# Decay attention and two expert layers on one core: weights' splitting paced by a count of VectorE's work, stores on GpSimd's queue, another order of the first expert layer's steps

## The chip, the cores and the metric

One NeuronCore of a Trainium2 chip runs the whole kernel. The metric is the device time of one execution in microseconds (us). The engines are named as in the profile: PE (TensorE), DVE (VectorE), ACT (ScalarE), POOL (GpSimd), SP (SyncE, which here only issues DMAs).

## What is computed

```python
def reference(q, k, v, s, w_in, w_out, w1, w2, w3, w_out2):       # cut
    scores = q @ k.T / sqrt(64)                  # 4 x 8 heads, 576 tokens, 64 wide
    cum = cumsum(max(s, 0));  bias = min(-(cum_i - cum_j), 0)
    attn = softmax(where(causal, -1e9, scores + bias)) @ v
    x = attn as (2304 tokens, 512)
    h = max(x @ w_in, 0)                         # 512 -> 2048
    x = (h * h) @ w_out                          # 2048 -> 512
    h = max(x @ w1, x @ w2, x @ w3)              # 512 -> 768 each
    return h @ w_out2                            # 768 -> 512
```

The weights arrive as 64-bit floats, the rest in 32 bits.

## The kernel before, in words

The order of every engine's instructions is the order in which the code emits them. There are three stages.

**Attention** works on 16 pairs of heads. A pair has nine units (tiles of scores), and a table (`ORDER`) says which step of which unit is emitted at each turn: scores on PE, mask and row maximum on DVE (line 673), exponential on ACT (line 687), transposes on PE and their copies on ACT (lines 729 to 754), the product with `v` on PE (line 774, tile `xv`), the row factors through DRAM (`r`, `px`, lines 704 to 713), the multiplication by them on POOL (line 792, tile `ax`) and the store of the pair's result on POOL's DMA queue (line 797, `x_at`). SP issues the loads of `xk`, `xq`, `ck`, `cq`, `xv`, and the small DMAs of `r` and `px`. Towards the end, `first_op` loads the first tokens of the next stage (`fx`, line 804), and ACT and DVE split them into a high and a low part (lines 810, 813); `FIRST_RAW` and `FIRST_OPS` say how many units ahead of the end of attention each of this is emitted.

**The weights** are prepared in jobs, by a class `Slots`, beside the attention and the first expert layer. A block of 128 x 512 64-bit words is loaded into a stage tile (`st`, line 379, two half loads), and four DVE operations of 512 elements (lines 386, 391, 395, 399) turn each word into a rounded 32-bit number and its rest; line 406 adds them. Where a layer uses sums of weights (a scheme with seven products in place of eight, lines 448 to 450), two blocks make one `sums` tile of seven parts. ACT makes the high part (lines 457, 419), DVE (POOL in attention) the low part by subtraction (lines 461, 422), and both are stored in DRAM (`keep_p`, lines 469 and 471; `keep`, line 426). PE's weights are then loaded from there into slots `sl` (lines 495, 498) by SP. A job is a list of stages; after each step of the main loop `pump` lets the open jobs go on by a credit of about one operation per step, whatever that operation's length. Weights' loads and stores are issued by SP in attention and by POOL after it (`queue`).

**The first expert layer** goes through 24 items; an item is a group of 768 tokens and a pair of blocks of the 2048 inner columns. It has seven products `p` (i = 0, 3, 2, 1, 4, 5, 6; six matmuls of 384 columns each, line 818) into two PSUM banks in turn (`first` in the trace), and eight output pieces `o` (three matmuls of 512 and three of 256 columns, line 1045), which belong to the item before. In `after`, ACT copies the banks after i = 0, 2, 1 into a tile `rr` (line 1006), DVE adds the banks after i = 3, 4, 5 to it (line 1017, called the rr addition below), ACT takes the maximum with zero, squares, and rounds to the high part (lines 1000, 996, 810), and DVE subtracts it for the low part (line 813, tile `hh`), which is emitted right behind the step. A product needs its bank read by the ACT or DVE operation of two products earlier, and an output piece needs both parts of `hh`. The products and pieces alternate:

```python
    for n in range(2, len(items1)):
        for c, i in enumerate(IN_ORDER):
            add_p(n, i)
            add_o(n - 1, pieces[c])
        add_o(n - 1, pieces[7])
```

**The second expert layer** and the output products (lines 818 and 1248) follow. No weights are prepared in it.

## Time and profile before

| | us |
|---|---|
| median of the two timed runs | 924.52 (923.7 and 925.33) |
| the profiled execution, its own time | 923.03 |
| its span in the trace | 921.3 |
| attention (to PE's last product of it) | 196.3 |
| first expert layer | 196.3 to 641.5 |
| second expert layer and output | 641.5 to 921.3 |

The 1.7 us between the profiled time and the span lie around the traced instructions. The stages are set apart by PE's products: its last product with the transposed row sums (line 777) starts at 196.1, its first products of the second expert layer at 640.1 and 641.5.

### The profile page before, as it was taken

The page shows a single profiled execution, that of the slowest core. Times are in us where ns is not written, and L with a number is a line of the kernel's source. Part 1 is how long each engine was busy: PE and PEld are TensorE (multiplying, and loading weights), DVE is VectorE, ACT ScalarE, POOL GpSimd, SP SyncE. Part 2 cuts the span into 40 slices and gives each one's busy share as a digit, 9 for nine tenths or more (in the row PEclk, how much of TensorE's full clock was granted, in tenths as well). Part 3 has the DMA queues.
Part 4 walks back from the last instruction along what each step waited for, and adds up shares of the span by engine and source line. Part 5 has one row for each costly group of instructions (what it writes and reads, how often), then busy time and mean ns, then how long its engine had stood idle before and what let it go on. Part 6 is the DMA issues. An engine that isn't in the chain of part 4 may idle for free.

```text
span 921.3 us, 16001 instructions
## 1 busy us (share of the span) xinstructions
PE 843.3 (92%) x5766; PEld 727.9 (79%) x5766; DVE 631.3 (69%) x1330; ACT 469.7 (51%) x981; POOL 182.8 (20%) x288
## 2 busy tenths in 40 slices
PE   8999968788887888989999989998799999999998
PEld 4655544467777877878999978986799999999998
DVE  7878758645876877777767776688245764676356
ACT  6898956755543544555555645553223442443224
POOL 2234241353132433322222212321000000000000
PEclk9999988988997999999999999999899999999999
DMA  4666867759786999945789837797983378246822
GB/s 145 201 180 214 274 190 246 226 160 386 243 298 238 345 320 354 334 166 201 263 289 329 303 105 259 248 385 273 384 306 144 113 277 278 96 144 194 315 71 69
DMA packets 89461, 220.28 MB, mean 239 GB/s; under 512 B 13480, under 2 KB 38120, under 8 KB 89384
## 3 DMA queue, kind: packets, MB, share of 16 engines
q1 hardware_dynamic: 69008, 150.06, 48.4%
q0 software_dynamic: 20352, 69.22, 20.6%
q8 instruction: 45, 0.74, 0.3%
q14 instruction: 32, 0.26, 0.1%
q10 hardware_dynamic: 24, 0.01, 0.0%
HBM read 158.22 MB, written 61.00 MB: 238 GB/s over the span
## 4 chain that ended last, share of the span: by engine, by line
PE 48%; DVE 18%; DMA 14%; ACT 8%; issue 8%; SPq 3%; POOL 2%; DVEq 0%; ACTq 0%; POOLq 0%
PE first L818 14%; PE banks L818 12%; PE banks L1045 7%; PE banks L1248 6%; DMA xq<-in_qT_dram 3%; PE pairs L774 3%; DVE xs L813 2%; DMA sl<-keep_p 2%; DMA st<-in_w_in_dram 2%; DVE rr L1017 2%; DMA px<-r 2%; DVE sums L448 1%; DVE sums L461 1%; DVE hh L813 1%; ACT xs L810 1%
## 5 line engine op out<-in xcount | busy, mean ns | idle before, releaser
L818 PE MATMUL first<-xs,sl 128*128 128x384 f32 x1350 | 279.5, 344 | 43.8 <-DVE rr L1017 27.4
L818 PEld LDWEIGHTS first<-xs,sl 128*128 128x128 f32 x1350 | 232.8, 191 | 51.5 <-DVE rr L1017 28.4
L1045 PE MATMUL banks<-hh,sl 128*128 128x512 f32 (+1 forms) x1152 | 235.3, 344 | 4.6 <-ACT hh L810 3.7
L1045 PEld LDWEIGHTS banks<-hh,sl 128*128 128x128 f32 x1152 | 199.5, 192 | 35.9 <-ACT hh L810 5.4
L818 PE MATMUL banks<-xs,sl 128*128 128x384 f32 x720 | 138.5, 338 | 0.2 <-DVE pt L1051 0.2
L818 PEld LDWEIGHTS banks<-xs,sl 128*128 128x128 f32 x720 | 125.7, 190 | 1.3 <-DVE c L1172 0.8
L1000 ACT ACTIVATE rr<-rr 128x384 f32<-128x384 f32 x69 | 36.3, 525 | 155.4 <-DVE rr L1017 155.4
L813 DVE TENSOR_TENSOR hh<-rr,hh 128x384 fp32r<-128x384 f32 (+1 forms) x69 | 47.7, 691 | 65.4 <-ACT hh L810 65.2
L687 ACT ACTIVATE e<-e,nm 128x128 f32<-128x128 f32 (+2 forms) x144 | 83.7, 585 | 16.9 <-DVE nm L673 16.7
L1248 PE MATMUL banks<-sl,hh 128*128 128x256 f32 x513 | 70.1, 283 | 1.7 <-DVE hh L813 1.4
L1248 PEld LDWEIGHTS banks<-sl,hh 128*128 128x128 f32 x513 | 66.8, 189 | 3.1 <-DVE hh L813 2.3
L774 PE MATMUL pairs<-et,xv 128*64 128x320 f32 (+4 forms) x448 | 56.5, 386 | 8.1 <-DMA xv<-in_v_main_dram 6.4
L774 PEld LDWEIGHTS pairs<-et,xv 128*64 128x64 f32 (+1 forms) x448 | 29.6, 142 | 42.2 <-issue 11.8
L1172 DVE TENSOR_TENSOR c<-banks,c 128x384 f32<-128x384 f32 x45 | 25.0, 555 | 47.1 <-PE banks L818 47.1
L813 DVE TENSOR_TENSOR xs<-xr,xs 128x768 fp32r<-128x768 f32 x44 | 42.7, 971 | 17.7 <-ACT xs L810 17.3
L729 PEld LDWEIGHTS pairs<-identF,e 64*128 64x128 f32 x800 | 35.4, 146 | 19.9 <-ACT et L751 8.8
L729 PE MATMUL pairs<-identF,e 64*128 64x64 f32 x800 | 42.8, 236 | 8.8 <-ACT et L751 5.9
L792 POOL TENSOR_TENSOR ax<-ax,px 128x256 f32<-128x256 f32 (+1 forms) x32 | 27.2, 850 | 92.5 <-DMA px<-r 84.2
L996 ACT ACTIVATE rr<-rr 128x384 f32<-128x384 f32 (+1 forms) x69 | 43.7, 633 | 2.2
L1017 DVE TENSOR_TENSOR rr<-first,rr 128x384 f32<-128x384 f32 x69 | 38.1, 553 | 8.9 <-PE first L818 7.4
L810 ACT CAST hh<-rr 128x384 fp32r<-128x384 f32 (+1 forms) x69 | 42.8, 621 | 2.2
L810 ACT CAST xs<-xr 128x768 fp32r<-128x768 f32 x44 | 36.7, 833 | 13.6 <-DVE xr L835 10.0
(140 smaller groups left out, 1176.2 us busy)
## 6 DMA issues: line engine op xcount, KB each, us to landing
sl<-keep_p SPq DMA_DIRECT2D x146, 512.0 KB
sl<-keep SPq DMA_DIRECT2D x35, 512.0 KB
keep_p<-hi POOLq DMA_DIRECT2D x18, 768.0 KB, 5.1
keep_p<-sums POOLq DMA_DIRECT2D x18, 768.0 KB, 6.1
st<-in_w_out_dram POOLq DMA_DIRECT2D x36, 256.0 KB, 5.8
st<-in_w_dram POOLq DMA_DIRECT2D x36, 256.0 KB, 5.5
keep<-wa POOLq DMA_DIRECT2D x28, 256.0 KB, 5.6
st<-in_w_in_dram POOLq DMA_DIRECT2D x20, 256.0 KB, 5.4
```

Of the source, the lines that this page charges most:

```text
L687: nc.scalar.activation(out=e_u[u][:, 0:w], in_=e_u[u][:, 0:w], func=ACTF.Exp, scale=-1.0, bias=st.pop(n), accum_out=sums[p, win][:, col:co ...
L729: nc.tensor.transpose(t[:, h, at * D:(at + 1) * D], e_u[v][rows(h), k * P:(k + 1) * P], identF[rows(h), rows(h)])
L774: nc.tensor.matmul(pv[rows(j), f:(W0, W1)[w]], lhsT=xv[0:kr, j, k, :], rhs=rhs, start=(k == 0), stop=(k == last))
L792: nc.gpsimd.tensor_tensor(out=x[:, 0:n], in0=x[:, 0:n], in1=rs_t.pop((p, w))[:, 0:n], op=ALU.mult)
L810: nc.scalar.copy(out=hi, in_=x)
L813: nc.vector.tensor_tensor(out=lo, in0=x, in1=f32(hi), op=ALU.subtract)
L818: nc.tensor.matmul(bank[:, 0:T2], lhsT=w[:, wp, at_w + kk * P:at_w + (kk + 1) * P], rhs=x[xp][:, kk, :], start=(start and kk == c == 0), s ...
L996: nc.scalar.activation(out=x, in_=x, func=ACTF.Square)
L1000: nc.scalar.activation(out=x, in_=x if src is None else src, func=ACTF.Relu)
L1017: nc.vector.tensor_tensor(out=x, in0=src, in1=x, op=ALU.add)
L1045: nc.tensor.matmul(dst[:, 0:hi_ - lo], lhsT=w[:, wp, d * P:(d + 1) * P], rhs=x[:, xp, lo:hi_], start=(c == 0 and key not in seen), stop=(l ...
L1248: nc.tensor.matmul(b, lhsT=hh[g, t, i][:, hp_, q, :], rhs=w[:, wp, at_w:at_w + DM // 2], start=(begin and n == c == 0 and i in ((0, 1, 3) ...
```

## The change

- In attention the weights' stores (high part first, low part later, as two steps) are issued by POOL's queue, no longer by SP's. The weights' loads stay on SP there.
- A job of the second weight matrix takes two blocks (column blocks q and q + 8) in place of one. Its stage tile holds both blocks (`st` 2 x 2 blocks in place of 3 x 1, `wa` 2 x 2 in place of 4 x 1). After attention, the four operations on the words, and that job's sum and low part, run over both blocks at once: 1024 elements. In attention they stay at 512.
- `pump` keeps a count of DVE's work (`work`): every DVE operation of the main loop adds 0.16 + 0.00104 per element, every weights' operation its `cost`; each step takes off 1.04; and a weights' operation is given out only while the count stays under 1.6 (1.9 when one is due soon).
- The low parts of the first expert layer are emitted two steps after their high parts, or ahead of the product that reads them.
- The order of products and pieces is one product, two pieces, two products, two pieces, and so on.
- There are 16 slots in place of 18; the order of the first weights' jobs, the number of open jobs (4 in place of 3), the steps without weights (3 in place of 6) and the start in attention (unit 6 in place of 9) are others; `FIRST_RAW` and `FIRST_OPS` load and split the first tokens 7 to 17 units earlier; the subtraction tile of the first tokens has a place of its own (`kept_raw`).

```diff
-SLOTS_A = 18
+SLOTS_A = 16
-FIRST_RAW = {0: -45, 1: -43, 3: -34, 2: -28}
+FIRST_RAW = {0: -62, 1: -60, 3: -47, 2: -36}
...
     def pump(self, time):
         self.clock += time
         if self.pos not in self.quiet or not self.phase:
             self.credit = min(self.credit % 1 + self.most, 4)
+            most = MOST_WORK
             if self.phase and any(self.due[job.i] < self.pos + URGENT for job in self.open):
                 self.credit += 1
+                most += 0.3
             for job in list(self.open):
                 while job in self.open and self.clock >= job.ready:
-                    free = job.stages[job.at].free
-                    if not free and self.credit < 1 or not self.step(job):
+                    stage = job.stages[job.at]
+                    if not stage.free and (self.credit < 1 or self.phase and self.work + stage.cost > most) or not self.step(job):
                         break
-                    self.credit -= not free
+                    if not stage.free:
+                        self.credit -= 1
+                        self.work += stage.cost
...
+        self.work = max(0.0, self.work - STEP)
...
     for n in range(2, len(items1)):
-        for c, i in enumerate(IN_ORDER):
-            add_p(n, i)
-            add_o(n - 1, pieces[c])
-        add_o(n - 1, pieces[7])
+        at = 0
+        for which, m in zip(((0,), (3, 2), (1, 4), (5, 6)), (2, 2, 2, 2) if n < len(items1) - 1 else (1, 2, 2, 3)):
+            add_p(n, *which)
+            add_o(n - 1, *pieces[at:at + m])
+            at += m
...
+        parts_ = (0, 1) if phase == 0 else (slice(0, 2),)
...
-            queue[0].dma_start(out=pairs[:, first // 2 + odd:first // 2 + odd + 3, h, :],
+            nc.gpsimd.dma_start(out=pairs[:, first // 2 + odd:first // 2 + odd + 3, h, :],
...
+        def flush(keep_n=None):
+            while lows and (keep_n is None or lows[0][0] <= keep_n):
+                low_of(*lows.pop(0)[2:])
...
-                later.append((x, hi, lo))
+                lows.append((now[0] + LOW_LATER, ("hh", n, f), x, hi, lo))
...
                 w = slots.get(("out", q + f * NQ1))
+                flush_for(("hh", n, f))
```

What moves is shown at three places. The first is PE's order in one item of the first expert layer before (`first` are the two banks of the products, `banks` those of the pieces, `sl` the weights):

```order
L818 MATMUL first_2950<-xs,sl_84 128x384 x6
L1045 MATMUL banks_3052<-hh_3070,sl_86 128x512 x3
L1045 MATMUL banks_3056<-hh_3070,sl_86 128x256 x3
L818 MATMUL first_2949<-xs,sl_87 128x384 x6
L1045 MATMUL banks_3053<-hh_3070,sl_86 128x512 x3
L1045 MATMUL banks_3056<-hh_3070,sl_86 128x256 x3
L818 MATMUL first_2950<-xs,sl_87 128x384 x6
```

and the same stretch now:

```order
L863 MATMUL first_2970<-xs,sl_83 128x384 x6
L1098 MATMUL banks_3072<-hh_3090,sl_97 128x512 x3
L1098 MATMUL banks_3076<-hh_3090,sl_97 128x256 x3
L1098 MATMUL banks_3073<-hh_3090,sl_97 128x512 x3
L1098 MATMUL banks_3076<-hh_3090,sl_97 128x256 x3
L863 MATMUL first_2969<-xs,sl_86 128x384 x6
L863 MATMUL first_2970<-xs,sl_86 128x384 x6
```

Two products now follow each other, then two pieces; between two products on the same bank there are still three other steps.

The second place is DVE's order in the first expert layer around the eighth item's first rr addition (`rr<-first`), before: lines 386 to 406, 448 and 461 are weights' work, line 813 the low parts.

```order
L1017 TENSOR_TENSOR rr_3073<-first_2950,rr_3073 128x384
L406 TENSOR_TENSOR sums_125<-st_119 128x512
L813 TENSOR_TENSOR hh_3070<-rr_3073,hh_3070 128x384
...
L813 TENSOR_TENSOR hh_3071<-rr_3074,hh_3071 128x768
L461 TENSOR_TENSOR sums_125<-sums_125,hi 128x896
L391 SCALAR_TENSOR_TENSOR st_120<-st_120,wa_123 128x512
L461 TENSOR_TENSOR sums_125<-sums_125,hi 128x896
L395 TENSOR_SCALAR wa_123<-st_120 128x512
L399 SCALAR_TENSOR_TENSOR st_120<-st_120,wa_123 128x512
L406 TENSOR_TENSOR wa_123<-st_120 128x512
L1017 TENSOR_TENSOR rr_3073<-first_2949,rr_3073 128x384
L813 TENSOR_TENSOR hh_3072<-rr_3073,hh_3072 128x384
```

The same place now:

```order
L1069 TENSOR_TENSOR rr_3093<-first_2970,rr_3093 128x384
L413 SCALAR_TENSOR_TENSOR st_117<-st_117,wa_120 128x1024
L858 TENSOR_TENSOR hh_3090<-rr_3093,hh_3090 128x384
L418 TENSOR_SCALAR wa_120<-st_117 128x1024
L858 TENSOR_TENSOR hh_3091<-rr_3094,hh_3091 128x768
L422 SCALAR_TENSOR_TENSOR st_117<-st_117,wa_120 128x1024
L505 TENSOR_TENSOR sums_121<-sums_121,hi 128x896 x2
L1069 TENSOR_TENSOR rr_3093<-first_2969,rr_3093 128x384
L427 TENSOR_TENSOR wa_120<-st_117 128x1024
L858 TENSOR_TENSOR hh_3092<-rr_3093,hh_3092 128x384
```

Between the low part of 768 and the rr addition stand three weights' operations in place of six, and between the rr addition and its low part stands one where there was none.

The third place is the queue of SP in attention, at the store of the first `sums` job, before:

```order
L704 DMA r_79<-rec 2x2x128
L469 DMA keep_p<-hi 128x3x512
L471 DMA keep_p<-hi 128x256
L469 DMA keep_p<-sums_125 128x3x512
L471 DMA keep_p<-sums_125 128x256
L713 DMA px<-r_80 64x320 x2
L622 DMA xv<-in_v_main_dram 128x2x256
```

Now these four stand in POOL's queue, there between the multiplications of the attention's results (line 836 now) and their stores (line 841 now):

```order
L513 DMA keep_p<-hi 128x3x512
L515 DMA keep_p<-hi 128x256
L505 TENSOR_TENSOR sums_121<-sums_121,hi 128x448 x3
L836 TENSOR_TENSOR ax<-ax,px 128x320
L841 DMA x_at_68<-ax 128x320
L505 TENSOR_TENSOR sums_121<-sums_121,hi 128x448
L513 DMA keep_p<-sums_121 128x3x512
L515 DMA keep_p<-sums_121 128x256
```

SP goes from `r` straight on to `px` and `xv`; three of the four low parts on POOL now stand in a row.

## Rows read from the trace of the kernel before

**Rows 1.** Windows: length, busy us of PE, PEld, DVE, ACT, POOL; clock, DMA share, GB/s.
```profile
100.00:196.30 96.30, 76.96 (x811) 44.06 (x807) 62.15 (x199) 62.66 (x156) 32.47 (x41) 0.88 0.68 215
196.30:420.00 223.70, 190.53 (x981) 169.77 (x980) 166.07 (x279) 108.52 (x191) 69.01 (x118) 0.95 0.82 291
420.00:641.50 221.50, 212.60 (x1188) 194.14 (x1187) 164.37 (x280) 121.73 (x212) 48.44 (x81) 1.00 0.75 265
641.50:921.30 279.80, 267.67 (x1695) 264.90 (x1695) 157.38 (x276) 94.68 (x205) 0.99 (x2) 0.99 0.58 201
```

**Rows 2.** PE's waits in the first expert layer: us in total, times, longest.
```profile
PE first L818 <- DVE rr L1017: 28.1, 20, 3.1
PE first L818 <- ACT rr L1006: 8.3, 12, 2.7
```

**Rows 3.** DVE's waits in the first expert layer.
```profile
DVE hh L813 <- ACT hh L810: 67.7, 56, 2.1
DVE xs L813 <- ACT xs L810: 8.9, 19, 1.3
DVE wa L386 <- DMA st<-in_w_out_dram: 7.7, 2, 5.4
```

**Rows 4.** PE's timeline: start, us, engine, line, operation, idle before and its releaser.
```profile
324.95 1.23 PE L818 MATMUL first<-xs,sl 128*128 128x384 f32 x6
326.02 1.22 PE L1045 MATMUL banks<-hh,sl 128*128 128x512 f32 x6
...
341.77 1.46 PE L818 MATMUL first<-xs,sl 128*128 128x384 f32 x5 [2.28 <-DVE rr L1017]
```

**Rows 5.** DVE's timeline ahead of that product.
```profile
336.77 1.08 DVE L461 TENSOR_TENSOR sums<-sums,hi 128x896 fp32r<-128x896 f32 x1
...
341.17 0.55 DVE L1017 TENSOR_TENSOR rr<-first,rr 128x384 f32<-128x384 f32 x1
343.41 0.56 DVE L813 TENSOR_TENSOR hh<-rr,hh 128x384 fp32r<-128x384 f32 x1 [1.69 <-ACT hh L810]
```

**Rows 6.** Groups by line and form: busy us, mean ns of one.
```profile
L399 DVE SCALAR_TENSOR_TENSOR st<-st,wa 128x512 f32<-128x512 uint32 x56 | 39.2, 700 | 1.0
L386 DVE TENSOR_SCALAR wa<-st 128x512 uint32<-128x512 uint32 x56 | 25.1, 449 | 17.5 <-DMA st<-in_w_out_dram 12.1 <-DMA st<-in_w_in_dram 4.8 <-issue 0.5
L1017 DVE TENSOR_TENSOR rr<-first,rr 128x384 f32<-128x384 f32 x69 | 38.1, 553 | 8.9 <-PE first L818 7.4 <-ACT rr L1006 1.5
L1176 DVE TENSOR_TENSOR res<-res,c 128x1152 f32<-128x1152 f32 x17 | 23.1, 1359 | 0.6
```

**Rows 7.** PE's timeline in attention: the first products of three pairs' last units.
```profile
81.58 1.08 PE L657 MATMUL pair<-xk,xq 64*64 64x512 f32 x4
91.18 1.08 PE L657 MATMUL pairs<-xk,xq 64*64 64x512 f32 x4
...
184.27 1.08 PE L657 MATMUL pair<-xk,xq 64*64 64x512 f32 x4
```

**Rows 8.** SP's timeline in attention: start of each issue, us that it took.
```profile
93.86 0.39 SPq L469 DMA_DIRECT2D keep_p<-hi  x1
...
95.84 1.24 SPq L471 DMA_DIRECT2D keep_p<-sums  x1
...
120.28 0.83 SPq L379 DMA_DIRECT2D st<-in_w_in_dram  x2
...
146.85 0.90 SPq L426 DMA_DIRECT2D keep<-wa  x2
...
150.17 1.10 SPq L471 DMA_DIRECT2D keep_p<-sums  x1
```

**Rows 9.** PE's longest wait between 100 and 196 us, in total.
```profile
PE pairs L774 <- DMA xv<-in_v_main_dram: 6.4, 3, 3.2
```

**Rows 10.** ACT's timeline at the longest of these.
```profile
132.72 0.83 ACT L810 CAST sl<-fx 128x768 fp32r<-128x768 f32 x1 [4.49 <-DMA fx<-x_at]
```

**Rows 11.** DVE's timeline in attention while POOL ran three subtractions.
```profile
122.53 2.89 DVE L697 TENSOR_SCALAR sm<-sm 128x5 f32<-128x5 f32 x1
```

More of the change, by code (lines that the diff above doesn't have):

```diff
@@ L132, in __init__, with busy, next_phase @@
         self.most = MOST[0]
-        self.keep_one = False
-        self.credit = 0.0
+        self.work = 0.0
+    def busy(self, n):
+        self.work += 0.16 + n * 0.00104
+    def next_phase(self, phase):
+        self.phase = phase
+        self.work = 0.0
+        for job in self.open:
+            job.ready = min(job.ready, self.clock + TIME)
     def next_use(self, i):
@@ L167, in step @@
         for room in set(room for room, _ in stage.take):
-            if len(self.rooms[room]) < sum(r == room for r, _ in stage.take) + (room == "st" and self.keep_one):
+            if len(self.rooms[room]) < sum(r == room for r, _ in stage.take) :
                 return False
@@ L408, in words_of, with power, rest @@
-        return ([Stage(lambda: load(0), take=(("st", "st" + x),), free=True), Stage(lambda: load(1), (6, 2), free=True)],
-                [Stage(exponent, take=(("wa", "wa" + x),)), Stage(cut_off, (0, 0.4)), Stage(power), Stage(rest, (1, 0.4))],
-                whole)
+        def power(x):
+            low, high, t = ops_on(x)
+            nc.vector.tensor_scalar(out=t, in0=high, scalar1=0xFF800000, scalar2=None, op0=ALU.bitwise_and)
+        def rest(x):
+            low, high, t = ops_on(x)
+            nc.vector.scalar_tensor_tensor(out=f32(low), in0=low, scalar=2.0 ** -52, in1=f32(t), op0=ALU.mult, op1=ALU.mult)
@@ new lines, in whole @@
+        def whole(out, x, eng):
+            low, high, _ = ops_on(x)
+            cut = (lambda y: y.rearrange("p (a c) -> p a c", a=2)) if len(out.shape) == len(low.shape) + 1 else (lambda y: y)
+            eng.tensor_tensor(out=out, in0=cut(f32(high)), in1=cut(f32(low)), op=ALU.add)
+        parts_ = (0, 1) if phase == 0 else (slice(0, 2),)
+        size = 512 if phase == 0 else 1024
+        ts, stt = 0.16 + size * 0.00054, 0.16 + size * 0.00104
+        loads_ = [Stage(lambda x=x, h=h: load(x, h), (6 * x * h, 3.3 * x * h), take=() if x or h else (("st", "st"),), free=True)
+                  for x in range(2) for h in range(2)]
@@ new lines, in both, with high_part, low_part, store @@
+        def both(x):
+            whole(f32(b["wa"][:, x]), x, adder[0])
+        def high_part(x):
+            nc.scalar.copy(out=hi_of()[:, x], in_=f32(b["wa"][:, x]))
+        def low_part(x):
+            adder[0].tensor_tensor(out=b["wa"][:, x].bitcast(F32R), in0=f32(b["wa"][:, x]), in1=f32(hi_of()[:, x]), op=ALU.subtract)
+        def store(x):
+            for y in range(2):
+                nc.gpsimd.dma_start(out=keep["out", q + y * NQ1][:, x * 512:(x + 1) * 512], in_=f32((b["wa"] if x else hi_of())[:, y]))
@@ new lines, in make @@
+        end = len(parts_) - 1
+        for n, x in enumerate(parts_):
+            stages.append(Stage(lambda x=x: both(x), (6 * (n == end), 0.4), give=(("st", "st"),) if n == end else (), cost=cost))
+        for x in range(2):
+            stages.append(Stage(lambda x=x: high_part(x), (3 * x, 0.4 + 0.4 * x), take=() if x else (("hi", "hi"),), free=True))
+        stages.append(Stage(lambda: store(0), free=True))
+        for n, x in enumerate(parts_):
+            stages.append(Stage(lambda x=x: low_part(x), (1, 0.4), cost=cost))
@@ L486, in make_sums @@
+        stages += [Stage(lambda: store(1), (4, 0.8), free=True), Stage(wait=(3, 0.8), give=(("hi", "hi"),), free=True),
+                   Stage(wait=(7, 0.4), give=(("sums", "sums"),), free=True), Stage(free=True)]
         return stages
@@ L834, in sub @@
             raw[key, out] = into
+        slots.busy(2 * T2)
         nc.vector.tensor_tensor(out=raw[key, out], in0=a, in1=b, op=ALU.subtract)
```

179 lines of the change are left out of this document (88 added, 91 removed).

## The prediction

> **What bounds the kernel now.** I read the windows by stage first, then PE's and DVE's waits in the stage that looked worst, then the timeline there, and last the timelines of attention.
>
> PE is the engine to watch. In the second expert layer it is busy 267.67 of 279.8 us at full clock, so nothing is to be had there, and nothing of the change works on it except for slots. In the first expert layer it is busy 190.53 + 212.60 = 403.1 of 445.2 us [rows 1]. Its own pace is faster than that: a step (six matmuls) starts 326.02 - 324.95 = 1.07 us after the one before where nothing waits [rows 4]; take 1.055, since pieces are a little shorter, and an item of 15 steps is 15.8 us and the 24 items 380 us. The stage lies 65 us above this floor: 445.2 - 403.1 = 42 of idle time and 23 of busy time at a lower clock (0.95 in the first half [rows 1]). The idle time is mostly one wait: 28.1 us in 20 places for the rr addition on DVE, and 8.3 us for ACT's copy of a bank [rows 2].
>
> So DVE is late in this stage, though it is busy only 166.07 + 164.37 = 330.4 us of it [rows 1]. The reader finds the rest in its waits: 67.7 + 8.9 = 76.6 us in which DVE stands at a low part until ACT has made the high part [rows 3]. Busy and blocked together are 407 us, more than PE's floor of 380. The timeline shows both sides of it: a run of weights' operations from 336.77 to 341.17, only then the rr addition, and behind it 1.69 us of standing still before its low part [rows 5]; PE waited 2.28 us for that addition [rows 4].
>
> In attention a pair takes 91.18 - 81.58 = 9.60 us where it runs freely, but the seven from 91.18 to 184.27 take 93.1 us, 25.9 more than 67.2 [rows 7]. There PE's clock is 0.88 [rows 1]. Where it waits, something from SP is late: `xv` 6.4 us in three places [rows 9], and ACT stood 4.49 us at the first tokens `fx` [rows 10], with all exponentials and copies behind it. SP spent 93.86 to 97.08 (four stores) and 146.85 to 151.27 (six stores) on weights' stores [rows 8], ahead of the `px` and `xv` of the running pair.
>
> **The change part by part.** All sums go against the profiled execution, 923.0 us; the median of the runs, 924.5, lies 0.2% above it.
>
> *Operations of 1024.* The trace has none. A two-input operation takes 553 ns at 384 and 1359 ns at 1152 elements [rows 6], so 1.05 ns per element and 0.15 us fixed; 1024 elements: 1.22 us, in place of 2 x 0.700 = 1.40. The one-input form takes 449 ns at 512; with the same fixed share two of them become 0.75 in place of 0.90. A pair of blocks has two of each: 2 x 0.18 + 2 x 0.15 = 0.66 us saved, and by the order 20 pairs run wide: 13 us of DVE's time. Bounds: nothing saved if time simply doubles; at best the wide one-input operation costs no more than the narrow one and the wide two-input one the 1.09 us of a line through 896 elements, about 30 us; and below nothing, since an rr addition that has become ready waits for the rest of a longer operation, 0.61 in place of 0.35 us on average, 0.26 x 20 places that PE waits for = 5 us. I take 13. Two blocks more are prepared in attention (12 in place of 10), and a few small ones fall out here: some 8 us more. DVE's work in the stage goes from 330 to about 309 us.
>
> *Low parts two steps later.* The 1.69 us in front of the low part [rows 5] is the time that ACT needs for maximum, square and rounding behind the rr addition. By DVE's new order a weights' operation of about 1.2 us stands in that gap, which leaves some 0.5: less than a third. 76.6 us fall to about 25, and 51 us of DVE's time come free. If no weights' operation is at hand, the wait stays; the order shows few such places in items 4 to 21. What is late next is the output piece that reads the low part, which comes four steps (4.2 us) after the product of i = 5.
>
> *The count.* Ahead of the rr addition at 341.17 stand six weights' operations, 4.4 us; the new order has three at that place, one of 1.22 and two of 1.09, 3.4 us, and the largest such run falls from 5.4 us to about 3.6. DVE's whole work per item, counted in the order with the rows' durations, is 17 to 20 us in items 2 to 7 before and 14.4 to 16.2 now; before it was 11 to 12 in items 12 to 16, where PE was at its floor anyway. So work moves from where DVE bounds to where it doesn't.
>
> *Sum for the stage.* DVE's account becomes 309 + 25 = 334 us against the floor of 380: PE bounds it, with single late additions left. I let 4 of the 28.1 us of waits for the rr addition stay, leave the 8.3 us on ACT's copies as they are, and let the slow clock go with the waits in their ratio (23 / 42 = 0.55): 24 x 1.55 = 37 us.
>
> *Products in twos.* Between two products on one bank there stay three steps, 3.2 us, so this is worth nothing by itself. It tightens two chains by one step each: ACT's copy after i = 2 now comes right behind the work of i = 3, and the first output piece one step sooner after i = 5. I cost that at nothing, with DVE's free time as its cover; without the cover it is the third rival.
>
> *Stores on POOL, attention.* SP loses 3.2 us and 4.4 us of issuing in the slow stretch [rows 8] and gains, by the order, eight more half loads of `st` at 0.83 / 2 us [rows 8], 3.3 us, less two slot loads of about that size: net 5 us earlier for what stands behind. The loads and splits of the first tokens are emitted 7 to 17 units earlier, and the wait of 4.49 us [rows 10] most likely goes: 5 us. Bounds: 26 us if every pair runs at 9.6, and a loss of 8 if POOL's queue, where a store now waits for ACT's high parts ahead of the multiplication by `px`, holds up `px`, and through its three buffers SP. Against it stand the low parts on POOL: DVE's 128 x 5 operation took 2.89 us while POOL ran three subtractions [rows 11], about one us for each, and by the order POOL gets 19 such operations on weights in place of 16: up to 3 us more, of which I count 2. So 8 us for attention.
>
> The Trainium skill (SBUF — State Buffer, "Who interferes with whom") says that VectorE and GpSimd share one pair of ports as an exclusive lock, the second to start waiting until the first has finished, and that a GpSimd-issued DMA's descriptors wait for it too. The 2.89 us row agrees with the first half. By that rule each added subtraction costs its whole time whenever DVE comes second, 3 us in place of 2; the second half no row here shows.
>
> *Slots, reloads.* By the order there are 12 more slot loads in the second expert layer and 6 in the first. The DMA share is 0.58 and 0.75 to 0.82 there [rows 1], and PE's waits name no weights: nothing, bounds -2 and +6 us.
>
> Sum: 923 - 37 - 8 = 878 us.
>
> **The rivals.**
>
> *Attention gains nothing or loses.* SP's queue is full whatever is taken from it, or POOL's queue holds up `px`. For it: the stretch had seven slow pairs, and only two of them stand behind stores. Against: the longest waits have named causes that move. With +3 in place of -8: 889 us.
>
> *Weights come late.* DVE waited 7.7 us in two places for `st<-in_w_out` [rows 3], in front of an rr addition; now a job loads four halves before it begins, on fewer tiles, in a stage that moves the same bytes in less time (291 GB/s at a share of 0.82 already [rows 1]). For it: that share. Against: eight steps now lie between load and first use where there were five. Price: twice those waits again, 15 us, on the path: 893 us.
>
> *The twos take back what the count gives (the slower end).* Call L the lateness of the rr addition. After i = 3, ACT's copy for i = 2 is done L + 2.6 us after the product, and i = 4 starts after 4.2: PE stands L - 1.6. The piece after i = 5 stands L - 2.0, the bank reuses twice L - 2.6. The rr addition at 341.17 was late by some 5 us (the three steps' 3.2 and 2.28 of wait, less its own 0.55) [rows 4, 5], so such L exist. With L = 3.2 throughout: 1.6 + 1.2 + 2 x 0.6 = 4.0 us per item, 88 us over 22 items, in place of the 18 us of idle left in the sum: 948 us. It is slower than before from L = 2.9 on. For it: weights' operations of 1.22 us can't be cut short. Against: the run ahead of an addition is shorter everywhere in the order, and DVE has 46 us to spare.
>
> *Half of it.* The wait at the low part goes, but PE's waits were set by bursts that remain: 12 of 28.1 us go with their clock, 19 us, attention keeps its time: 904 us.
>
> **How the numbers follow.** The forecast, 878 us with 862 to 890 of its own, gets 0.58 (some of it below 862); attention without gain 0.13; late weights 0.11; half of it 0.11; the twos 0.07. A measurement of this kernel tells about 2% from no change: below 905 is faster, above 941 slower. The first three cases and a little of the half are faster: 0.82; the rest of the half and the rivals' tails 0.11; the twos 0.07. The range, 856 to 907, leaves out the twos at the top and an attention at its full 26 us at the bottom.
>
> **What would show it.** Right: DVE's waits at low parts at 15 to 35 us in the first expert layer, PE's waits for rr additions under 10, items at 16 to 17 us, that stage at 400 to 415 us; the first group's `fx` without a wait; attention ending at 183 to 193. Wrong: PE's waits for ACT's copies (the rr tiles) over 20 us, which is the third rival; DVE waiting for `st` over 15 us, the second; `ax` on POOL late behind a store, and pairs still at 13 us and more, the first.

## The result, and the profile after

The changed kernel took 879.51 us in the median of two runs (876.66 and 882.36) against 924.52: a ratio of 0.9513, 95% interval 0.9376 to 0.9651. Timed again in five runs beside the kernel before, it took 877.17 us, ratio 0.9500 (0.9476 to 0.9524). The forecast was 878.0.

The profiled execution took 876.7 us with a span of 874.7. Its windows by stage answer to [rows 1] (length, busy us of PE, PEld, DVE, ACT, POOL; clock, DMA share, GB/s):

```profile
100.00:190.79 90.79, 75.73 (x852) 43.87 (x848) 69.53 (x217) 66.27 (x166) 37.92 (x48) 0.94 0.73 239
190.79:400.00 209.21, 193.79 (x1057) 174.36 (x1056) 162.22 (x240) 118.61 (x222) 67.31 (x111) 0.98 0.86 311
400.00:599.77 199.77, 196.27 (x1113) 179.84 (x1112) 152.85 (x227) 114.09 (x215) 47.31 (x76) 1.00 0.83 306
599.77:874.70 274.93, 267.73 (x1696) 264.97 (x1695) 154.94 (x271) 94.83 (x205) 0.00 (x0) 0.99 0.63 216
```

Attention ends at 190.8 in place of 196.3 (-5.5), the first expert layer takes 409.0 in place of 445.2 (-36.2), the second 274.9 in place of 279.8 (-4.9): together 46.6 us, the difference of the two spans. PE is busy 390.1 of the 409.0 us, at a clock of 0.98 and 1.00 where it was 0.95 and 1.00.

PE's and DVE's waits in the first expert layer, after (us in total, times, longest), answer to [rows 2, 3]:

```profile
PE first L863 <- ACT rr L1057: 10.5, 13, 1.5
PE first L863 <- DVE rr L1069: 6.4, 4, 3.2
```

```profile
DVE hh L858 <- ACT hh L854: 45.3, 42, 2.0
DVE xs L858 <- ACT xs L854: 10.2, 16, 2.4
...
DVE wa L408 <- DMA keep<-wa: 5.9, 2, 5.1
DVE sums L427 <- DMA keep_p<-sums: 3.7, 1, 3.7
```

The wait for the rr addition fell from 28.1 us in 20 places to 6.4 in four. DVE's wait at low parts fell less: from 76.6 to 55.5 us, not to 25. The last two rows are new: DVE stands in front of a weights' operation until a store has read the tile that it is about to write. The longest of them was on the path: behind it came an rr addition, and PE waited for that. The timelines of DVE and of PE:

```profile
353.99 0.69 DVE L408 TENSOR_SCALAR wa<-st 128x1024 uint32<-128x1024 uint32 x1 [5.10 <-DMA keep<-wa]
```

```profile
357.61 2.23 PE L863 MATMUL first<-xs,sl 128*128 128x384 f32 x6 [3.20 <-DVE rr L1069]
```

When the changed kernel was run again, DVE stood nearly as long at this operation, but the last to come was the load of its stage tile, not a store:

```profile
357.62 0.70 DVE L408 TENSOR_SCALAR wa<-st 128x1024 uint32<-128x1024 uint32 x1 [4.88 <-DMA st<-in_w_dram]
```

So a late store and a late load end close together here. In the first execution the DMA engines were 0.99 busy from 253 to 339 us, just ahead of this place (371 GB/s); whether that makes both late was not tried.

The wide operations, by line and form, have the estimated durations (busy us, mean ns of one): 1.22 us with two inputs and 0.69 to 0.70 with one, where 1.22 and 0.75 were taken.

```profile
L422 DVE SCALAR_TENSOR_TENSOR st<-st,wa 128x1024 f32<-128x1024 uint32 x20 | 24.4, 1220 | 0.1
L418 DVE TENSOR_SCALAR wa<-st 128x1024 uint32<-128x1024 uint32 x20 | 14.0, 698 | 0.2
```

### The profile page after: what moved, and what is told of

The parts are those of the page before. It is cut to its first block, busy times and chain, and to the rows that moved or that the text cites. A ratio compares the mean times of both kernels' runs of the same rounds, so it can differ in the third digit from the quotient of the medians.

```text
span 874.7 us, 16004 instructions
## 1 busy us (share of the span) xinstructions
PE 826.9 (95%) x5766; PEld 716.4 (82%) x5766; DVE 623.7 (71%) x1241; ACT 473.1 (54%) x1015; POOL 193.3 (22%) x295
## 4 chain that ended last, share of the span: by engine, by line
PE 54%; DVE 14%; DMA 13%; ACT 10%; issue 5%; POOL 2%; SPq 1%; DVEq 0%; ACTq 0%; POOLq 0%
PE first L863 16%; PE banks L863 13%; PE banks L1098 10%; PE banks L1300 7%; PE pairs L818 3%; DMA keep_p<-sums 2%; ACT rr L1047 2%; DMA xq<-in_qT_dram 2%; DVE rr L1069 2%; DMA xv<-in_v_main_dram 2%; ACT hh L854 2%; DMA keep<-wa 2%; DVE xs L858 2%; ACT rr L1051 1%; DMA st<-in_w_out_dram 1%
## 5 line engine op out<-in xcount | busy, mean ns | idle before, releaser
L863 PE MATMUL first<-xs,sl 128*128 128x384 f32 x1350 | 265.5, 339 | 18.8 <-ACT rr L1057 10.5
L863 PEld LDWEIGHTS first<-xs,sl 128*128 128x128 f32 x1350 | 231.8, 189 | 26.4 <-ACT rr L1057 15.9
L1098 PE MATMUL banks<-hh,sl 128*128 128x512 f32 (+1 forms) x1152 | 219.0, 339 | 1.9 <-ACT hh L854 0.7
L1098 PEld LDWEIGHTS banks<-hh,sl 128*128 128x128 f32 x1152 | 187.9, 189 | 30.3 <-DVE hh L858 3.1
L818 PE MATMUL pairs<-et,xv 128*64 128x320 f32 (+4 forms) x448 | 53.8, 372 | 8.6 <-DMA xv<-in_v_main_dram 7.7
L858 DVE TENSOR_TENSOR xs<-xr,xs 128x768 fp32r<-128x768 f32 x44 | 42.6, 970 | 21.2 <-ACT xs L854 18.7
```

The source lines that it names most:

```text
L818: nc.tensor.matmul(pv[rows(j), f:(W0, W1)[w]], lhsT=xv[0:kr, j, k, :], rhs=rhs, start=(k == 0), stop=(k == last))
L858: nc.vector.tensor_tensor(out=lo, in0=x, in1=f32(hi), op=ALU.subtract)
L863: nc.tensor.matmul(bank[:, 0:T2], lhsT=w[:, wp, at_w + kk * P:at_w + (kk + 1) * P], rhs=x[xp][:, kk, :], start=(start and kk == c == 0), s ...
L1098: nc.tensor.matmul(dst[:, 0:hi_ - lo], lhsT=w[:, wp, d * P:(d + 1) * P], rhs=x[:, xp, lo:hi_], start=(c == 0 and key not in seen), stop=(l ...
```

## The experiments

Twelve runs, in three groups; each group was timed beside the kernel before. In the table, "end" is the start of the first expert layer, "layer 1" its length and "rest" what follows, all from the profiled executions. "Account" is DVE's busy time in the layer plus its waits for ACT's high parts (of tokens, hidden values and weights), to be held against PE's floor of 380. The floor is the prediction's estimate; PE is busy for 389 us or more of the layer in every run.

```
run                      us      ratio (95%)               end    layer 1  rest   account
before                   924.52  1                         196.3  445.2    279.8  410
changed                  879.51  0.9513 (0.9376, 0.9651)   190.8  409.0    274.9  373
changed, again           877.17  0.9500 (0.9476, 0.9524)   193.8  410.3    273.3  377
lows at once             908.44  0.9833 (0.9798, 0.9868)   194.3  439.0    275.0  418
old credit               905.63  0.9793 (0.9751, 0.9834)   191.7  428.8    279.0  394
narrow operations        889.63  0.9621 (0.9553, 0.9690)   190.3  423.0    273.6  388
one by one               885.06  0.9559 (0.9512, 0.9606)   188.5  416.4    273.6  383
before, lows later       913.59  0.9883 (0.9848, 0.9919)   195.1  439.2    280.0  390
old credit, later reuse  883.15  0.9577 (0.9548, 0.9606)   191.6  415.9    277.3  377
later reuse              884.31  0.9581 (0.9562, 0.9601)   194.3  415.1    273.1  374
stores on SP             883.51  0.9568 (0.9545, 0.9592)   193.6  412.7    273.0  374
lows three               883.44  0.9571 (0.9536, 0.9607)   191.7  416.5    275.5  352
lows three, split        870.81  0.9448 (0.9423, 0.9474)   193.6  403.2    275.1  349
weights on DVE           873.46  0.9474 (0.9447, 0.9502)   186.8  406.6    275.4  376
```

**Low parts at once.**

```diff
-LOW_LATER = 2
+LOW_LATER = 0
```

> The changed kernel (876.7 us in its profiled execution, first expert layer 409.0 us) with every low part in the step right behind its high part, as before the change. If the delay of the low parts carries the gain: DVE's waits at low parts, 55.5 us in this stage of the changed kernel, go back to about 80, with 315 us of work that is 395 us against PE's floor of 380, PE's waits for rr additions rise from 6.4 to 15-20 us, the stage takes 422-432 us and the kernel 890-900. If the count and the wider operations carry it: DVE has room for the longer waits, PE's waits for rr additions stay under 9 us, the stage takes 409-413 us and the kernel 877-881.

Measured: 31 us slower than the changed kernel (0.9833 against 0.9500 of 922 us). DVE's and PE's waits in the first expert layer:

```profile
DVE hh L858 <- ACT hh L854: 89.5, 65, 2.1
DVE xs L858 <- ACT xs L854: 12.9, 21, 2.1
```

```profile
PE first L863 <- ACT rr L1057: 18.1, 22, 1.5
PE first L863 <- DVE rr L1069: 15.9, 17, 2.2
```

DVE stands 102.4 us in place of 55.5, its account is 418, and the layer is back at 439.0. In the changed kernel most of the gain hangs on the delay of the low parts. It costs more to undo than expected: with wide operations and the count, a low part at once leaves DVE standing longer than before the change (76.6).

**Old credit in place of the count.**

```diff
-MOST = (1, 1, 1)
-MOST_FIRST = 1
+MOST = (1, 0.5, 1)
+MOST_FIRST = 0.55
...
-MOST_WORK = 1.6
+MOST_WORK = 99.0
...
-                self.credit += 1
+                self.credit += 0.5
```

> The changed kernel without the count of VectorE's work: weights' operations are given out by the old credit, at half its rate since an operation is twice as wide (0.5 a step, 0.55 in the first items, 0.5 more where urgent). By the order DVE's work per item is then 14.6 to 18.4 us in items 2 to 7 (14.4 to 16.2 with the count) and 10 to 11 us in items 12 to 16 (13.5 to 14.7), the longest run of weights' operations ahead of an rr addition 3.8 us in place of 3.6, but only 15 additions have over 2 us ahead of them in place of 32. If the count carries part of the gain: items 4 to 7 take 18-20 us, PE's waits for rr additions are 12-18 us, the stage 417-424 us, the kernel 885-892. If it carries none, because DVE has room in every item: PE's waits for rr additions 4-8 us, the stage 405-410 us, the kernel 873-878.

Measured: 27 us slower than the changed kernel, so the count looked worth that much. But PE waited no longer for rr additions than with the count:

```profile
PE first L863 <- DVE rr L1069: 5.5, 6, 2.2
```

What PE waited for was ACT: POOL's store of the high parts, ACT's timeline and PE's timeline show the worst place:

```profile
276.81 0.91 POOL L513 DMA_DIRECT2D keep_p<-hi  x1
```

```profile
288.61 0.62 ACT L454 CAST hi<-wa 128x512 fp32r<-128x512 f32 x1 [8.93 <-DMA keep_p<-hi]
```

```profile
289.66 2.29 PE L863 MATMUL first<-xs,sl 128*128 128x384 f32 x6 [8.27 <-ACT rr L1057]
```

The weights' high parts have one tile, `hi`. ACT stood in its queue 8.93 us until a store had read it, with the copy of a bank behind it. It did so in two more places (7.11 and 3.80 us), and PE lost 8.27, 4.58 and 2.02 us there. This was neither of the two theories; it got a run of its own (below).

**Narrow operations.**

```diff
-MOST = (1, 1, 1)
-MOST_FIRST = 1
+MOST = (1, 2, 1)
+MOST_FIRST = 2
...
-        parts_ = (0, 1) if phase == 0 else (slice(0, 2),)
-        size = 512 if phase == 0 else 1024
+        parts_ = (0, 1)
+        size = 512
```

> The changed kernel with weights' operations of 512 in the first expert layer too (two a step allowed, the count unchanged). By the order DVE's work on weights rises from 190.6 to 206.4 us. If the wide operations matter only through DVE's account: 315 + 16 + 55 of waits = 386 us against PE's floor of 380, so little is lost: stage 411-417 us, kernel 879-885. If each us of DVE's work stands on the path: 16 us more, 893. If the shorter operations let an rr addition start sooner, and that outweighs the work: stage 403-407 us, kernel 871-875.

Measured: 11 us slower than the changed kernel, between the first two theories. PE's waits for rr additions even fell to 2.7 us; what came instead were a piece's weights that were late and an ACT standing at `hi`. PE's waits in the layer:

```profile
PE banks L1098 <- DMA sl<-keep: 7.2, 1, 7.2
PE banks L1098 <- ACT hh L854: 5.1, 2, 4.4
```

DVE's work rose by 8.4 us (315.1 to 323.5), not by the 16 expected. So what the narrow operations cost PE showed at weights and at `hi`, and not at rr additions; why these came late was not tried apart.

**One by one on PE.**

```diff
-        at = 0
-        for which, m in zip(((0,), (3, 2), (1, 4), (5, 6)), (2, 2, 2, 2) if n < len(items1) - 1 else (1, 2, 2, 3)):
-            add_p(n, *which)
-            add_o(n - 1, *pieces[at:at + m])
-            at += m
+        for c, i in enumerate(IN_ORDER):
+            add_p(n, i)
+            add_o(n - 1, pieces[c])
+        add_o(n - 1, pieces[7])
```

> The changed kernel with the old order on TensorE, a product and an output piece in turn, in place of twos. If the twos cost nothing and gain nothing, as forecast: PE's waits for ACT's copies stay near 10.5 us in 13 places, the kernel takes 874-880 us. If the twos tighten the copy: those waits fall under 5 us and the kernel takes 868-873. If the twos give slack that the additions use (two pieces stand between an addition and the next product on its bank): PE's waits for rr additions rise from 6.4 to over 12 us and the kernel takes 883-890.

Measured: 885.06 us, 5 us above the changed kernel, with intervals that overlap. Both mechanisms are there and trade against each other: PE's waits for ACT's copies fall from 10.5 to 3.7 us (they were 7.8 when the changed kernel was run again), those for rr additions rise from 6.4 to 10.4 (7.0 again). These two nearly cancel. PE's longest wait, 4.14 us for ACT's `hh`, is of another kind: as with the old credit, ACT stood at the tile `hi`:

```profile
323.89 1.14 ACT L453 CAST hi<-wa 128x512 fp32r<-128x512 f32 x2 [7.14 <-DMA keep_p<-hi]
```

So the 5 us can't be put down to PE's order as such.

**The low parts alone, in the kernel before.**

```diff
+LOW_LATER = 2
...
-                later.append((x, hi, lo))
+                lows.append((now[0] + LOW_LATER, ("hh", n, f), x, hi, lo))
...
-                    while later:
-                        low_of(*later.pop(0))
-                    flush()
+                    flush(k)
```

> The kernel before with one part of the change: low parts two steps later. If that part carries most of the gain by itself (undoing it alone cost the changed kernel some 30 us): DVE's waits at low parts in the first expert layer fall from 76.6 us to 50-55, its account from 407 to about 383 us against PE's floor of 380, PE's waits for rr additions from 28.1 to 8-14 us, the stage from 445.2 to 418-428 us, the kernel takes 897-908. If it works only where the count has evened out DVE's work: PE's waits for rr additions stay over 20 us, the kernel takes 914-922.

Measured: 913.59 us, 9 to 11 us faster than before, and only 6 of them in this layer. DVE's waits:

```profile
DVE hh L814 <- ACT hh L811: 36.1, 38, 1.7
...
DVE wa L423 <- ACT wa L420: 10.0, 6, 2.2
...
DVE sums L462 <- ACT hi L458: 8.7, 7, 2.5
```

The wait for tokens' and hidden values' high parts falls by 35 us (76.6 to 41.3), but DVE now comes sooner to the weights' own low parts and stands 18.7 us there (3.2 before). The account falls only from 410 to 390, still above the floor of 380, and PE's waits for rr additions only from 28.1 to 23.4 us. In the changed kernel the weights' jobs let steps pass between high and low part, and that wait is 2.8 us. The delay needs the rest of the change in order to pay in full.

**Old credit with later reuse.**

```diff
-Stage(lambda: store(1), (4, 0.8), free=True)
+Stage(lambda: store(1), (4, 2.4), free=True)
```

(In both kinds of job, on top of the run with the old credit.)

> The run without the count (old credit), with the tile of the high parts given back four steps later and the tiles of sums and words four later with it. In the run without the count ACT stood 8.93, 7.11 and 3.80 us in front of a weights' high part until a store had read that tile, and PE stood 8.27, 4.58 and 2.02 us behind it. If what the count gave was mostly that distance between jobs: these waits fall under 5 us together, the stage from 428.8 to 410-416 us, the kernel takes 883-890. If it was the evening out of DVE's work (15 to 18.7 us per item in items 1 to 5 here): those waits go but PE's waits for rr additions rise over 12 us, the stage stays at 422-430 us, the kernel takes 896-904.

Measured: 883.15 us. Of the 27 us that the missing count cost, 20 come back when `hi` and the other tiles are held some steps longer; no wait of ACT for a store over 2 us is left, and PE's waits for rr additions stay short although items 1 to 5 carry by the order 15 to 18.7 us of DVE's work:

```profile
PE first L863 <- DVE rr L1069: 8.9, 9, 2.2
```

Most of what the count gave was the distance between jobs. Some 3 of the 7 us that stay lie in the rest (277.3 us), since the last job ends in the second expert layer (which starts at 607.5; that job's last store is issued at 622.4). One thing is not apart: holding tiles longer also spread DVE's work. Between the last rr additions of one item and the next it was 16.1, 16.5, 16.8 and 17.2 us in four items in a row with the old credit alone, and 17.7, 13.8, 14.9 and 12.6 in the same items here.

**Later reuse in the changed kernel.**

```diff
-Stage(lambda: store(1), (4, 0.8), free=True), Stage(wait=(3, 0.8), give=(("hi", "hi"),), free=True)
+Stage(lambda: store(1), (4, 2.0), free=True), Stage(wait=(3, 1.6), give=(("hi", "hi"),), free=True)
```

(In both kinds of job.)

> The changed kernel with its count, the tile of the high parts given back three steps later and those of sums and words five later. In the changed kernel DVE stood 5.10 and 3.74 us in front of weights' operations until a store had read their tile, and PE waited 3.20 us for the rr addition behind the first. If those two waits are on the path: they go, the stage falls from 409.0 to 402-406 us, the kernel takes 868-873. If they are covered or come back in another place: 875-881. If the jobs end too late for their first use: weights' operations in a burst ahead of a product, over 885.

Measured: 884.31 us, 7 above the changed kernel. DVE's two waits for stores went (2.5 us left), and PE's in the layer became

```profile
PE banks L1098 <- DMA sl<-keep: 9.1, 2, 5.3
```

With tiles held longer, two blocks of output weights are late for their first use, which costs more than the waits for stores did. Beside the run before it, this is also the fairest test of the count: with tiles held longer in both, by nearly the same steps, the kernel takes 884.31 us with the count (0.9581) and 883.15 without it (0.9577). The count then gives nothing that can be measured.

**Stores back on SP in attention.** One of the three lines; the other two alike:

```diff
-            nc.gpsimd.dma_start(out=pairs[:, first // 2 + odd:first // 2 + odd + 3, h, :],
+            queue[0].dma_start(out=pairs[:, first // 2 + odd:first // 2 + odd + 3, h, :],
```

> The changed kernel with the weights' stores of attention back in SP's queue. If moving them gave what was forecast (net 5 us earlier for what stands behind them in SP's queue): attention ends at 195-197 in place of 190.8, the kernel takes 880-886. If SP's queue is full either way: attention ends at 189-192, the kernel takes 875-880. If the stores in POOL's queue held up more than they freed: attention ends before 188 and the kernel takes 868-873.

Measured: 883.51 us, 6 above the changed kernel, as expected, but not where expected. Attention ended at 193.6; nine executions of this table with the same attention ended between 188.5 and 194.3, 191.9 in the mean. Of the loss, some shows just behind it, in PE's and in DVE's timeline: a slot load and the next tokens are late.

```profile
205.53 4.92 PE L863 MATMUL first<-xs,sl 128*128 128x384 f32 x18 [3.34 <-DMA sl<-keep_p]
```

```profile
225.86 0.96 DVE L858 TENSOR_TENSOR xs<-xr,xs 128x768 fp32r<-128x768 f32 x1 [6.13 <-DMA xr<-x_at]
```

SP's timeline gives its first slot load of the stage, in this run and then in the changed kernel, which stood 2.4 us for those tokens and not at all for the slot:

```profile
200.98 0.53 SPq L539 DMA_DIRECT2D sl<-keep_p  x1
```

```profile
195.90 0.53 SPq L539 DMA_DIRECT2D sl<-keep_p  x1
```

SP comes to it 7.4 us after the stage's start (200.98 - 193.59) in place of 5.1 (195.90 - 190.79): its queue is some 2 us fuller when attention ends. In the other runs of the table with the stores on POOL the same distance is 4.8 to 5.3 us, so this part is no scatter.

**The changed kernel again.** No edit.

> The changed kernel as it is, timed in more rounds, as the base for the other runs: its two runs gave 876.66 and 882.36 us. If its time is that of the runs with stores in SP's queue, with the old credit and later reuse, or with later reuse (883 to 884 us), none of these three parts moved the time by more than can be measured; if it is 877 or less, each is worth some 6 us. Expected 880.

Measured: 877.17 us (874.31 to 879.45). Against this base the stores (0.9545 to 0.9592) and the old credit with later reuse (0.9548 to 0.9606) are slower by 6 and 7 us; later reuse too.

**Low parts three steps later.**

```diff
-LOW_LATER = 2
+LOW_LATER = 3
```

> The changed kernel with low parts one step later still (three in place of two). By the order the longest run of weights' operations ahead of an rr addition falls from 3.6 to 3.1 us and 18 additions in place of 32 have over 2 us ahead of them. If standing at low parts still takes time that DVE needs: those waits fall from 55.5 us to 30-38, PE's waits for rr additions and ACT's copies from 16.9 us to 8-12, the stage from 409.0 to 400-405, the kernel takes 868-874. If what is left of the waits is time that DVE has to spare: they fall but the kernel takes 876-882. If the low part is now too late for the output piece: PE waits over 4 us for DVE's hh in front of pieces, the kernel takes over 883.

Measured: 883.44 us, 6 above the changed kernel. DVE's waits at low parts fall to 37.6 us and its account to 352, but PE now stands in front of output pieces:

```profile
PE banks L1098 <- DVE hh L858: 6.3, 3, 3.2
```

In the changed kernel that wait was 0.7 us (2.2 when run again). The two longest of these, 3.18 and 2.46 us, come behind an idle DVE: it stood 2.97 and 3.32 us until a stage tile was loaded, with the low part queued behind it. The first:

```profile
331.56 0.69 DVE L408 TENSOR_SCALAR wa<-st 128x1024 uint32<-128x1024 uint32 x1 [2.97 <-DMA st<-in_w_out_dram]
```

A third wait of PE, 3.10 us, comes behind ACT, which stood 5.73 us at `hi`. So the loss comes from late weights and the tile `hi`; a low part with less slack lets them through to PE. Whether DVE's 18 us of shorter waits were worth something, this run can't tell; the next one, with the same low parts, has the shortest layer of all.

**The same, with the half loads of `st` split in attention.**

```diff
-    loads_ = [Stage(lambda x=x, h=h: load(x, h), (6 * x * h, 3.3 * x * h), take=() if x or h else (("st", "st"),), free=True)
+    loads_ = [Stage(lambda x=x, h=h: load(x, h), (6 * x * h + 2 * h * (1 - x), 3.3 * x * h), take=() if x or h else (("st", "st"),), free=True)
```

> As the run with low parts three steps later, and in attention the four half loads of a job are issued in two twos, two units apart. In the changed kernel SP issued four of them in 3.52 us from 139.36, ahead of r, px and xv of the running pair, and PE waited 5.48 us for xv at 150.65; the runs with later reuse and with stores in SP's queue waited 5.21 and 4.06 us in the same place. If that block of issues makes xv late: that wait falls under 2 us, attention ends 3 to 4 us earlier and the kernel takes 3 to 4 us less than the run without the split. If xv is late for another reason (its buffer, or transfers ahead of it): no difference beyond 2 us.

Measured: 870.81 us, 0.9448 (0.9423 to 0.9474): faster than the kernel before, and its interval lies just below that of the changed kernel. But the reason for which it was tried fell. SP's timeline, PE's timeline and a window of the same stretch:

```profile
139.03 1.58 SPq L539 DMA_DIRECT2D sl<-keep_p  x3
140.70 1.38 SPq L399 DMA_DIRECT2D st<-in_w_out_dram  x2
...
143.46 0.56 SPq L666 DMA_DIRECT2D xv<-in_v_main_dram  x1
```

```profile
151.47 1.55 PE L818 MATMUL pairs<-et,xv 128*64 128x256 f32 x8 [4.75 <-DMA xv<-in_v_main_dram]
```

```profile
140.00:152.00 12.00, 6.91 (x73) 3.77 (x74) 8.33 (x24) 8.89 (x24) 3.35 (x5) 0.91 0.95 315
```

`xv` is issued 1.8 us sooner than in the changed kernel (143.46 against 145.29) and PE waits nearly as long (5.48 us there, 4.60 when it was run again): it lands some 8 us after its issue, behind three slot loads of 512 KB and two half loads of 256, with the DMA engines 0.95 busy. The issues ahead of it are not what makes it late; the bytes ahead of it are what is left, which was not tried by itself. The gain lies in the first expert layer (403.2 against 416.5 without the split), where jobs begin at other steps than in the run without it, and PE's wait for `hh` is under 1 us. Which of these steps does it was not tried, nor the split with low parts two steps later.

**Weights' sums and low parts on DVE in attention.**

```diff
-    adder = [nc.gpsimd]
+    adder = [nc.vector]
```

> The changed kernel with GpSimd's sums and low parts of weights in attention given to DVE: 19 operations of 448 or 512 elements, 0.61 to 0.70 us each there, so 12 us more of DVE's 153.7 us of work in 190.8 us. If GpSimd's operations hold up DVE's small ones (PE waited 2.64 and 1.74 us for DVE's nm while GpSimd ran low parts) by more than DVE's own work costs: those two waits go and attention ends at 185-189, the kernel takes 873-878. If DVE has no 12 us to give in attention: nm and rec late in more places, attention ends at 195-201, the kernel takes 884-891.

Measured: attention ends at 186.8, before all of those nine (188.5 at the earliest); 873.46 us, 0.9474 (0.9447 to 0.9502), some 2 to 4 us below the changed kernel, with intervals that overlap. The place that was in question, in the changed kernel on POOL and on DVE, and then on DVE in this run:

```profile
55.72 3.33 POOL L505 TENSOR_TENSOR sums<-sums,hi 128x448 fp32r<-128x448 f32 x3
59.00 0.85 POOL L836 TENSOR_TENSOR ax<-ax,px 128x320 f32<-128x320 f32 x1
```

```profile
56.14 4.01 DVE L418 TENSOR_SCALAR wa<-st 128x512 uint32<-128x512 uint32 x1
```

```profile
56.14 0.40 DVE L418 TENSOR_SCALAR wa<-st 128x512 uint32<-128x512 uint32 x1
```

Behind the 4.01 us PE waited 2.64 us for DVE's `nm`. That wait is gone, and the 12 us of added work found room. The end of attention stands on one execution.

## Why the prediction was right, and where not

**The bound.** DVE's lateness held PE in the first expert layer. PE's waits for rr additions went from 28.1 to 6.4 us with the change, and 15.9 came back when low parts were emitted at once. The accounts of the table fit this in part: the five above 385 have the five longest layers (423 to 445 us). But in two of the five, old credit and narrow operations, PE waited only 5.5 and 2.7 us for rr additions, and its long waits came from `hi` and late weights; there the account fits without being the cause. Below 380 it no longer orders the runs: 352 goes with a layer of 416.5 us, 349 with 403.2.

**The stage's sum** of 37 us came out at 36.2, with 18.9 us of PE's idle time left where the sum left 18, and 10 us of slow clock. But one step in it was mis-sized: "76.6 us fall to about 25". It was 55.5, the account 371 and not 334 (373 in the table, which counts the weights' high parts too). That this did no harm fits the account, since 371 is still under 380. It is not shown further: with three steps the wait fell to 37.6 us, but that run lost its time to late weights and to `hi`.

**Wide operations.** Their durations were right to 0.06 us, DVE's work fell to 315 us where 309 were forecast. Undoing them cost 11 us, but at late weights and at `hi`, for which the sum had no term.

**The count.** The step "work moves from where DVE bounds to where it doesn't" is not what it does. Without it and with tiles held longer, the kernel ran within 7 us of the changed one and level with the one that had both. What the count mainly keeps apart are jobs that share one `hi` tile and two others; neither the sum nor a rival spoke of these tiles.

**Low parts and the rest.** The sum added the parts. Alone, the low parts gave 9 to 11 us; undone, they cost 31. Undone one at a time, the five parts that were tried cost 31, 27, 11, 6 and 5 us, 80 together, where the whole change gives 45.

**The twos** at nothing: undoing them cost 5 us with overlapping intervals. PE's waits for ACT's copies were 10.5 us (7.8 when run again), not over 20, so the third rival fell.

**Attention** was to give 8 us and gave 5.5 in the profiled execution, 3.8 by the mean of nine ends (191.9) against the mean of the two with the old attention (195.7: the kernel before, and the kernel before with low parts later). The wait for `fx` went from 4.49 to 2.3 us and did not vanish, that for `xv` went from 6.4 to 7.7. Moving the stores back cost 6 us, but attention's end did not show it; part of it lies at the start of the next stage. The earlier first tokens, the 16 slots and the earlier start of the weights were not undone, so which part moved attention's end is not shown.

**Weights late**, the second rival, did not decide the result, but it is there: DVE's waits for `st` were 1.9 us in the changed kernel, 8.2 when it was run again, and 15.9 with low parts three steps later. PE paid for late weights in that run (5.6 us), with tiles held longer (9.1) and with narrow operations (7.2).

**The change of stage** was missing from the sum: 4.9 us. Before the change, the last job's low parts stood ahead of the last additions on DVE and its stores just ahead of the result's on the DMA engines. POOL's, SP's and ACT's timelines of the kernel before:

```profile
641.17 0.75 POOL L469 DMA_DIRECT2D keep_p<-sums  x1 [0.57 <-DVE sums L461]
```

```profile
644.11 1.20 SPq L1133 DMA_DIRECT2D x_mid<-rr  x1
```

```profile
649.46 0.48 ACT L1180 COPY res<-first 128x384 f32<-128x384 f32 x1 [10.47 <-DMA x_mid<-pt]
```

SP's and ACT's timelines of the changed kernel, whose last weights' store is issued at 564.9:

```profile
600.05 0.39 SPq L1182 DMA_DIRECT2D x_mid<-rr  x1
```

```profile
602.20 0.48 ACT L1231 COPY res<-first 128x384 f32<-128x384 f32 x1 [10.34 <-DMA x_mid<-pt]
```

From issue to copy 5.3 us became 2.2, and PE's wait 7.15 became 1.76. It follows how shortly before the end of the layer the last of these stores is issued: 2.6 us before it with the old credit (617.96 of 620.55) it was 5.48 us, 9.6 us before it with later reuse as well (597.95 of 607.53) 3.18 us. These two runs also tell the stores from the additions held up on DVE. With the old credit the additions were in time, and SP's last issue came 0.3 us after the layer's end as in the changed kernel, but the copy 5.8 us behind it:

```profile
620.88 1.18 SPq L1182 DMA_DIRECT2D x_mid<-rr  x1
```

```profile
626.70 0.48 ACT L1231 COPY res<-first 128x384 f32<-128x384 f32 x1 [12.31 <-DMA x_mid<-pt]
```

With later reuse as well it is the other way round: weights' work stood among the last additions, the issue came 1.7 us after the layer's end (609.26), the copy 2.1 us behind it (611.39). Before the change there were both: 2.6 us to the issue, where now it is 0.3, and 5.3 to the copy. So some 2.3 us were the additions and 3.2 the stores.

**The total** of 46 us came from -5.5, -36.2 and -4.9 where -8, -37 and 0 were forecast. That the shortfall in attention and the missing term cancel to within 3 us is luck; the stage's term is not, though its account was off by 37 us on the way. Of the signs on record, the stage's length, the waits for rr additions and attention's end came out; DVE's waits at low parts (55.5 us against 15 to 35) and the first group's `fx` (2.3 us against none) did not.

## What to carry to other kernels

Add the busy time of the engine that looks idle to the time that it stands at its own partners, and hold the sum against the pace of the engine that should bound; as long as it lies above, waits of that engine are worth taking away; below it the sum no longer tells which of two kernels is faster. Look at which wait PE stood in, too: a sum can agree where another wait took the time. When work for a later stage is spread into an earlier one, its few tiles are a resource like an engine's time: a wait for a store in an in-order queue holds all that stands behind it. Undo one part at a time, and also make one alone: the two values can differ by a factor of three.

## What the runs showed of the hardware that was not expected

A DVE operation did not get in between GpSimd operations that stood one behind another. The 0.40 us operation above took 4.01 us, from inside the first of three subtractions to just past the multiplication behind them (56.14 to 60.15 against 55.72 to 59.85); [rows 11] show the same with three. The prediction's price of about one us for each fits; that it is paid in a row where GpSimd's operations stand in a row had not been drawn from them. Not every DVE operation stands so: in the kernel before, one that reads scores from PSUM (line 673, 128x384) took 0.56 us inside such a subtraction and 0.52 us just after the last. The Trainium skill (SBUF — State Buffer, "Who interferes with whom") says, of operations that need the ports shared by the two engines, that whoever issues first has them for its whole instruction and the other fully blocks; the 4.01 us row agrees and goes further, since three more instructions of GpSimd began and ended while DVE's stood.
